# Transposes on TensorE, a regrouped first FFN2 and other buffers in the last chunk of a fused attention and SwiGLU kernel

## The chip, the cores and the metric

The kernel runs on one core of a Trainium2 chip. The metric is device time in microseconds (us), as a median over executions of the whole program. Executions of one kernel mostly agree within about 1%, but some fall into a slower state (345.35 us against 335.1 for the kernel before). Each run also reports the mean clock granted to TensorE, as a share of full speed.

## The reference, cut to what matters

```python
# q, k, v: (8 batches, 8 heads, 576 positions, 64)
scores = 0.125 * q @ k.T, kept where |i - j| <= 32
attn   = softmax(scores) @ v
x      = attn laid out as (4608 tokens, 512)
out    = (silu(x @ w_gate) * (x @ w_val)) @ w_out      # d_ff = 1536
```

## The kernel before

The 4608 tokens are 36 pairs of 64-row windows (a "pair" is 128 tokens) and 9 chunks of 512 tokens (four pairs each), numbered from 0. For each chunk TensorE computes FFN1 (12 units of gate and value products), then FFN2. Attention of later pairs is threaded into FFN2. Chunk 0's FFN2 is plain; chunks 1 to 8 use a seven-product scheme with the steps p1, p2, p6, p5, p7, p3, p4, which needs sums of blocks of `hT` (on VectorE) and of `w_out` (on GpSimd, once). Each pair's attention output `x16` has to be transposed into `xT` before FFN1 of its chunk can start.

```python
def pair_mask(m):                       # VectorE, both operands in SBUF
    nc.vector.tensor_tensor(out=flat, in0=flat, in1=mask, op=ALU.mult)

def pair_xt(m, on_pe=False, pool=None, cast=None):
    ...
    if not on_pe:
        nc.sync.dma_start_transpose(out=dst, in_=x16)
        return
    ...                                 # four TensorE transposes, then a copy out of PSUM

# end of the first FFN2
ffn2_sub(0, 3, 0); pair_xt(4, True, ...); pair_xt(5, True, ...)
ffn2_sub(0, 3, 1); pair_xt(6, True, ...); pair_xt(7, True, ..., cast_dve)
pair_av(8); pair_xt(8); load_v(2, range(5))
wino_weights()                          # GpSimd: 4 subtractions and 2 casts of 128x1536

# last chunk (split): x in ps_a (two buffers, also used by FFN1), z in ps_c (one buffer)
# outputs: tiles "osb2", 3 buffers
for j in range(1, NCH):
    ffn1(j)
    if j == NCH - 2: good = check_range()
    if j == NCH - 1: set_flag(good)     # 'cnt' in ps_c, read by VectorE into 'flag'
    ffn2(j, ...)
```

Each engine works through its instructions in the order of the program: in the changed kernel's trace the copy of `xT` starts at 63.63, behind a mask product on VectorE, though the transposes that it reads ended at 58.84. The flag decides at the end whether a slow general path must run; it never does here.

## Time and profile before

| | kernel before |
|---|---|
| median time | 335.27 us (335.13 to 345.35, 3 runs) |
| span of the profiled execution | 333.8 us |
| TensorE busy | 312.6 us, 94% |
| TensorE waits on transposed x | 4.1 us, at the starts of chunks 2, 3, 4 |
| first FFN2 | 44.06 to 60.64 us |
| last output copy ends | 328.01 us |
| granted clock | 0.992 |

TensorE carries the kernel from start to end, so the places that matter are those where it stands still with work left. The prediction shows those lines. Columns are start, duration (us), engine, source line, operation, result and operands.

```profile
55.29 0.69 DVE L316 TENSOR_TENSOR p_t<-p_t,mask 128x1024 f16<-128x1024 f16 x1 [1.61 <-ACT p_t L312]
56.36 3.12 POOL L457 TENSOR_TENSOR w_top<-wo 128x1536 f16<-128x1536 f16 x1
```

In the kernel before, pair 8's mask is done at 55.98, just 0.4 us before GpSimd starts on the weight sums, which last until 71.9.

### The profile page before, as it was taken

How to read it: one execution, taken by the hardware profiler on the slowest of the kernel's cores; microseconds unless marked ns; L12 is line 12 of the kernel's file. 1: busy time of each engine (PE TensorE's matmuls, PEld its weight loads, DVE VectorE, ACT ScalarE, POOL GpSimd, SP SyncE). 2: the span in 40 equal slices, each digit the busy share in tenths (PEclk: the TensorE clock that was granted, in tenths of full speed). 3: DMA queues.
4: the chain of work that ended last, by engine and by line, in shares of the span. 5: the costliest groups of instructions: out<-in, count | busy, mean ns of one | idle time of the engine just before them, and what ended most of it. 6: DMA issues, size and time to landing. Idle time of an engine off the chain costs nothing. (4 is left out here: it accounts for less than half of the span.)

```text
span 333.8 us, 7176 instructions
## 1 busy us (share of the span) xinstructions
PE 312.6 (94%) x2868; PEld 181.1 (54%) x2868; DVE 201.6 (60%) x409; ACT 162.2 (49%) x247; POOL 121.1 (36%) x145
## 2 busy tenths in 40 slices
PE   6789998999989998999799999999999999899990
PEld 3444554445844584448444864486448644754480
DVE  3743366347846684868477767686668566634740
ACT  3864579476743475337433753374337623223320
POOL 8972888997405620355046403460000000000000
PEclk9999999999999999999999999999999999999996
DMA  7999999869989998999699979997621510020012
GB/s 278 173 210 304 217 162 186 145 99 141 130 171 140 116 100 190 116 140 120 159 130 146 102 163 121 152 120 157 115 53 33 141 33 1 33 94 1 2 66 69
DMA packets 157000, 41.96 MB, mean 126 GB/s; under 512 B 140576, under 2 KB 154400, under 8 KB 156960
## 3 DMA queue, kind: packets, MB, share of 16 engines
q0 software_dynamic: 100640, 16.52, 68.8%
q1 hardware_dynamic: 56320, 24.92, 32.5%
q8 instruction: 24, 0.39, 0.5%
q14 instruction: 16, 0.13, 0.1%
HBM read 37.75 MB, written 9.44 MB: 141 GB/s over the span
## 5 line engine op out<-in xcount | busy, mean ns | idle before, releaser
L423 DVE TENSOR_TENSOR hT<-ssb,gv_ps 128x512 f16<-128x512 f16 x108 | 74.3, 688 | 92.0 <-ACT ssb L422 91.6
L422 ACT ACTIVATE ssb<-gv_ps 128x512 f16<-128x512 f32 x108 | 64.5, 597 | 123.5 <-PE gv_ps L416 121.8
L416 PE MATMUL gv_ps<-xT,wg 128*128 128x512 f16 x432 | 111.0, 380 | 5.3 <-DMA xT<-x 4.1
L416 PE MATMUL gv_ps<-xT,wv 128*128 128x512 f16 x432 | 110.9, 379 | 0.0
L416 PEld LDWEIGHTS <-wg 128*128 128x128 f16 x432 | 41.3, 98 | 53.4 <-issue 6.1
L416 PEld LDWEIGHTS <-wv 128*128 128x128 f16 x432 | 42.3, 98 | 51.0
L223 POOL DMA_DIRECT2D tok<-in_q_dram x30 | 25.5, 849 | 64.2 <-DMA qT<-tok 45.7
L312 ACT ACTIVATE p_t<-s_ps 128x1024 f16<-128x1024 f32 (+1 forms) x40 | 34.8, 924 | 13.3 <-PE s_ps L306 13.3
L223 POOL DMA_DIRECT2D tok<-in_k_dram x30 | 25.3, 842 | 15.9 <-DMA kT<-tok 13.1
L499 PEld LDWEIGHTS <-hT 128*128 128x128 f16 x288 | 27.6, 98 | 5.7 <-issue 0.7
L499 PEld LDWEIGHTS <-s_top 128*128 128x128 f16 x288 | 27.6, 98 | 4.8 <-DVE s_top L471 1.1
L386 DVE TENSOR_TENSOR x<-o_ps,rall 128x512 f16<-128x512 f32 (+1 forms) x39 | 25.4, 650 | 1.3
L499 PE MATMUL x_ps<-w_top,s_top 128*128 128x256 f16 x192 | 23.8, 273 | 0.9 <-DVE s_top L471 0.9
L316 DVE TENSOR_TENSOR p_t<-p_t,mask 128x1024 f16<-128x1024 f16 x32 | 20.9, 687 | 4.2 <-ACT p_t L312 3.5
L242 POOL DMA_DIRECT2D v<-in_v_dram x24 | 21.3, 902 | 0.5 <-DMA tok<-in_q_dram 0.5
L471 DVE TENSOR_TENSOR s_top<-hT 128x768 f16<-128x768 f16 (+2 forms) x48 | 20.1, 418 | 0.0
L265 DVE COPY v<-v 64x512 f16<-64x512 f16 x46 | 15.5, 337 | 1.4
L685 ACT ACT_TABLE_LOAD x12 | 15.4, 1283 | 0.2
L368 PEld LDWEIGHTS <-p_t 128*64 128x64 f16 x576 | 10.7, 110 | 6.6 <-issue 4.7
L368 PE MATMUL o_ps<-v,p_t 128*64 128x66 f16 x576 | 12.9, 196 | 0.7 <-DVE p_t L352 0.7
L527 DVE TENSOR_TENSOR osb<-y_ps,kept 128x512 f32<-128x512 f32 (+1 forms) x16 | 10.5, 655 | 4.8 <-ACT p_t L312 4.0
L262 ACT ACTIVATE kept<-x_ps 128x512 f32<-128x512 f32 (+1 forms) x18 | 9.6, 531 | 6.9 <-PE x_ps L499 6.9
(81 smaller groups left out, 270.8 us busy)
## 6 DMA issues: line engine op xcount, KB each, us to landing
out_dram<-osb SPq DMA_DIRECT2D x32, 256.0 KB, 2.5
v<-in_v_dram POOLq DMA_DIRECT2D x24, 128.0 KB, 5.2
tok<-in_q_dram POOLq DMA_DIRECT2D x24, 128.0 KB, 5.0
tok<-in_k_dram POOLq DMA_DIRECT2D x24, 128.0 KB, 5.5
qk_st<-in_q_dram SPq DMA_DIRECT2D x4, 576.0 KB, 7.0
qk_st<-in_k_dram SPq DMA_DIRECT2D x4, 576.0 KB, 8.9
v<-in_v_dram POOLq DMA_DIRECT2D x16, 96.0 KB, 5.2
wo<-in_moe_w_out_dram POOLq DMA_DIRECT2D x4, 384.0 KB, 21.5
```

Source lines behind the costliest of these rows:

```text
L223: nc.gpsimd.dma_start(out=t[0:n].rearrange("p (h d) -> p h d", d=D), in_=src[b].rearrange("h s d -> s h d")[128 * m:128 * m + n])
L242: nc.gpsimd.dma_start(out=dst[:, 2 * m, :, 0:D], in_=src[128 * m - 32:128 * m + 96])
L265: nc.vector.tensor_copy(out=o, in_=i)
L312: nc.scalar.activation(out=o, in_=s, func=AF.Exp, bias=0.0, scale=1.0 / float(D) ** 0.5)
L316: nc.vector.tensor_tensor(out=flat, in0=flat, in1=mask, op=ALU.mult)
L368: nc.tensor.matmul(out=o[h // 4][64 * i:64 * i + 64, 66 * (h % 4):66 * (h % 4) + 66], lhsT=p[:, place(b, h)[0], i, place(b, h)[1], :], rhs ...
L386: nc.vector.tensor_tensor(out=x16s[m][:, a], in0=ov[:, :, :, 0:D], in1=r.unsqueeze(3).to_broadcast([128, a.stop - a.start, 4, D]), op=ALU. ...
L416: nc.tensor.matmul(out=gv[:, i, :], lhsT=w[:, g, 128 * fk:128 * fk + 128], rhs=xts[j][:, g, :], start=(g == 0), stop=(g == GS - 1))
L422: nc.scalar.activation(out=ssb, in_=gv[:, 0, :], func=AF.Silu, bias=0.0, scale=1.0)
L423: nc.vector.tensor_tensor(out=hts[j][:, fk, :], in0=ssb, in1=gv[:, 1, :], op=ALU.mult)
L471: tt = lambda o, a, b, op: nc.vector.tensor_tensor(out=o, in0=a, in1=b, op=op)
L499: nc.tensor.matmul(out=dst[n], lhsT=lhs[:, f, 128 * n:128 * n + 128], rhs=rhs[:, f, :], start=(first and f == 0 and (split or n == 0)), st ...
```

## The change

The intent has three parts. Transposes that are urgent at the end of chunks 1 to 3 go to TensorE in place of the DMA. The attention inside the first FFN2 is regrouped so that no copy is waited for. The last chunk gets PSUM buffers that FFN1 doesn't hold, and eight output buffers (for room, its `kept` tiles are joined; not shown).

```diff
+        tp = pool.tile([128, len(ms), GS, 128], FP16, tag=..., name="xt_ps")
+        for n, x in enumerate(x16):
+            for g in range(GS):
+                nc.tensor.transpose(out=tp[:, n, g, :], in_=x[:, 128 * g:128 * g + 128], identity=ident)
+        cast(dst.rearrange("p g (n t) -> p n g t", t=128), tp)
 ... last chunk
-            x = [ps_a.tile([128, 256], FP32, tag="a", name="x_ps") for _ in range(2)]
+            x2 = ps_c.tile([128, 2, 512], FP32, tag="c", name="x_ps")
-            z2 = ps_c.tile([128, 2, 512], FP32, tag="c", name="z_ps")
+            z = [ps_a.tile([128, 256], FP32, tag="a", name="z_ps") for _ in range(2)]
-                               tag="osb" if n is None else "osb2", name="osb")
+                               tag="osb" if n is None else "osb2", name="osb",
+                               bufs=3 if n is None else 8)
 ... first FFN2 (the earlier groups are cut)
-    pair_scores(8)
+    pair_scores(7, ps_c)
+    ex8 = pair_scores(8, None, False)          # not masked here
+    ex8()
+    ffn2_sub(0, 2, 1)
     nc.scalar.activation(... dummy, Silu ...)
-    ffn2_sub(0, 2, 1)
-    pair_av(6)
-    pair_av(7, ps_a)
+    turn_x([4, 5, 6], ps_a, cast_act)
     ffn2_sub(0, 3, 0)
-    ... (four transposes of pairs 4 to 7)
+    pair_av(7)
+    pair_mask(8)
     ffn2_sub(0, 3, 1)
-    ...
-    pair_av(8)
-    pair_xt(8)
+    turn_x([7], ps_a, cast_dve)
 ... ends of chunks 1 to 3
+        urgent = {1: (1, 2), 2: (1, 2), 3: (1,)}.get(j, ())
         st["p3"]()
+        if urgent:
+            turn_x([todo[i] for i in urgent], ps_a, cast_dve)
         st["c12"]()
```

More of the change, by code (lines that the diff above doesn't have):

```diff
@@ L389, in pair_norm, with pair_xt, turn_x @@
                                     op=ALU.mult)
-    def pair_xt(m, on_pe=False, pool=None, cast=None):
-        j, i4 = divmod(m, 4)
+    def pair_xt(m):
+        turn_x([m], None)
+    def turn_x(ms, pool, cast=None):
+        j, i4 = divmod(ms[0], 4)
         if j not in xts:
             xts[j] = xtpool.tile([128, GS, 512], FP16, tag="xt", name="xT")
-        dst = xts[j][:, :, 128 * i4:128 * i4 + 128]
-        x16 = x16s.pop(m).rearrange("p a h d -> p (a h d)")
-        if not on_pe:
-            nc.sync.dma_start_transpose(out=dst, in_=x16)
+        dst = xts[j][:, :, 128 * i4:128 * (i4 + len(ms))]
+        x16 = [x16s.pop(m).rearrange("p a h d -> p (a h d)") for m in ms]
+        if pool is None:
+            nc.sync.dma_start_transpose(out=dst, in_=x16[0])
             return
-        pool, tag = pool or (ps_o, "o")
-        tp = pool.tile([128, GS, 128], FP16, tag=tag, name="xt_ps")
-        for g in range(GS):
-            nc.tensor.transpose(out=tp[:, g, :], in_=x16[:, 128 * g:128 * g + 128],
-                                identity=ident)
-        (cast or cast_act)(dst, tp)
+        tp = pool.tile([128, len(ms), GS, 128], FP16,
+                       tag={ps_a: "a", ps_c: "c", ps_o: "o"}[pool], name="xt_ps")
+        for n, x in enumerate(x16):
+            for g in range(GS):
+                nc.tensor.transpose(out=tp[:, n, g, :], in_=x[:, 128 * g:128 * g + 128],
+                                    identity=ident)
+        cast(dst.rearrange("p g (n t) -> p n g t", t=128), tp)
     hts = {}
@@ L481, in wino_steps @@
         if split:
-            x = [ps_a.tile([128, 256], FP32, tag="a", name="x_ps") for _ in range(2)]
+            x2 = ps_c.tile([128, 2, 512], FP32, tag="c", name="x_ps")
+            x = [x2[:, 0, 0:256], x2[:, 1, 0:256]]
             y = [ps_o.tile([128, 256], FP32, tag="o", name="y_ps") for _ in range(2)]
-            z2 = ps_c.tile([128, 2, 512], FP32, tag="c", name="z_ps")
-            z = [z2[:, 0, 0:256], z2[:, 1, 0:256]]
+            z = [ps_a.tile([128, 256], FP32, tag="a", name="z_ps") for _ in range(2)]
             parts = (0, 1)
@@ L504, in keep_act @@
         def keep_act(name, src):
+            t = opool.tile([128, 2, 256], FP32, tag="kept", name="kept", bufs=3)
             for n in parts:
-                t = kept[(name, n)] = opool.tile([128, 2, 256] if n is None else [128, 256], FP32,
-                                                 tag="kept" if n is None else f"kept{n}",
-                                                 name="kept", bufs=3)
-                cast_act(t, views(src, n))
+                kept[(name, n)] = t if n is None else t[:, n]
+                cast_act(kept[(name, n)], views(src, n))
         def send(n, o, i, c):
@@ L634 @@
     for m in range(4):
-        pair_xt(m, True)
+        turn_x([m], ps_o, cast_act)
     c16 = [cast_qk(t, cast_pool) for t in st]
@@ L650 @@
     ffn2_sub(0, 0, 0)
-    pair_scores(4)
-    pair_scores(5)
-    ffn2_sub(0, 0, 1)
     shift_v(1, 0, cast_dve)
     shift_v(1, 1, cast_dve)
-    ffn2_sub(0, 1, 0)
+    pair_scores(4, ps_c)
+    pair_scores(5)
     pair_scores(6)
-    pair_scores(7)
+    ffn2_sub(0, 0, 1)
     shift_v(1, 2, cast_act)
     shift_v(1, 3, cast_act)
+    ffn2_sub(0, 1, 0)
     load_qk(2)
@@ L664 @@
     pair_av(5, ps_a)
+    pair_av(6, ps_a)
     ffn2_sub(0, 2, 0)
-    pair_scores(8)
+    pair_scores(7, ps_c)
+    ex8 = pair_scores(8, None, False)
+    ex8()
+    ffn2_sub(0, 2, 1)
     nc.scalar.activation(out=dummy, in_=rall[0:1, 0, 0:1], func=AF.Silu, bias=0.0, scale=1.0)
-    ffn2_sub(0, 2, 1)
-    pair_av(6)
-    pair_av(7, ps_a)
+    turn_x([4, 5, 6], ps_a, cast_act)
     ffn2_sub(0, 3, 0)
-    pair_xt(4, True, (ps_a, "a"))
-    pair_xt(5, True, (ps_a, "a"))
+    pair_av(7)
+    pair_mask(8)
     ffn2_sub(0, 3, 1)
-    pair_xt(6, True, (ps_a, "a"))
-    pair_xt(7, True, (ps_a, "a"), cast_dve)
-    pair_av(8)
-    pair_xt(8)
+    turn_x([7], ps_a, cast_dve)
     load_v(2, range(5))
     wino_weights()
-    carried = []
+    carried = [8]
     def table(func):
@@ L736, in norm @@
                 pair_norm(todo[i])
-                pair_xt(todo[i])
+                if i not in urgent:
+                    pair_xt(todo[i])
         if n:
```

## The prediction

> **What bounds the kernel now.** I first read busy time by engine on the page, then who TensorE waits for, then the order of time around each wait.
>
> ```profile
> PE 312.6 (94%) x2868; PEld 181.1 (54%) x2868; DVE 201.6 (60%) x409; ACT 162.2 (49%) x247; POOL 121.1 (36%) x145
> ```
>
> TensorE is busy 312.6 of 333.8 us; no other engine passes 60%. Busy is not the same as peak, but it says that time can be won only where TensorE stands still, or after its last matmul. The view of waits for TensorE lists all such places with a releaser:
>
> ```profile
> PE gv_ps L416 <- DMA xT<-x: 4.1, 3, 1.7
> PE warm L552 <- DVE mask L202: 2.9, 1, 2.9
> PE gv_ps L416 <- ACT xT L262: 1.1, 2, 0.7
> PE xt_ps L403 <- DVE x L386: 0.9, 1, 0.9
> ```
>
> The change aims at lines 1, 3 and 4 (2 is the start, untouched). The timeline shows the three waits of line 1 at the start of FFN1 of chunks 2, 3, 4; here are the first and last:
>
> ```profile
> 91.65 1.47 PE L499 MATMUL x_ps<-ws_rest,hT 128*128 128x256 f16 x12
> 94.34 1.02 PE L416 MATMUL gv_ps<-xT,wg 128*128 128x512 f16 x4 [1.22 <-DMA xT<-x]
> ...
> 160.35 1.47 PE L499 MATMUL x_ps<-ws_rest,hT 128*128 128x256 f16 x12
> 163.50 0.81 PE L416 MATMUL gv_ps<-xT,wg 128*128 128x512 f16 x3 [1.67 <-DMA xT<-x]
> ```
>
> A product of 12 matmuls takes 1.31 us from its start to the next one's (289.28 onward in the chain), so the gaps are 94.34 - 91.65 - 1.31 = 1.38, for chunk 3 (126.00 to 128.67) 1.36, and 163.50 - 160.35 - 1.31 = 1.84 us: 4.58 together. Chunks 5 to 8 show none of size there.
>
> The first FFN2 runs from 44.06 to 60.64 and waits twice near its end:
>
> ```profile
> 57.72 0.40 PE L403 MATMUL xt_ps<-ident,x 128*128 128x128 f16 x4 [0.92 <-DVE x L386]
> 57.96 1.46 PE L430 MATMUL ob<-wo,hT 128*128 128x512 f16 x6
> 59.25 0.61 PE L403 MATMUL xt_ps<-ident,x 128*128 128x128 f16 x8
> 59.79 0.45 PE L368 MATMUL o_ps<-v,p_t 128*64 128x66 f16 x16
> 60.64 1.02 PE L416 MATMUL gv_ps<-xT,wg 128*128 128x512 f16 x4 [0.40 <-ACT xT L262]
> ```
>
> The tail, around the last chunk's first product and its last outputs:
>
> ```profile
> 315.37 0.19 PE L571 MATMUL cnt<-ones,good 128*1 128x1 f32 x2
> 315.49 0.83 PE L499 MATMUL x_ps<-wo,hT 128*128 128x256 f16 x6
> 316.85 0.81 PE L499 MATMUL x_ps<-wo,hT 128*128 128x256 f16 x6 [0.53 <-DVE hT L423]
> 317.38 0.14 DVE L572 TENSOR_SCALAR flag<-cnt 1x1 int32<-1x1 f32 x1
> 324.05 1.48 PE L499 MATMUL x_ps<-ws_rest,hT 128*128 128x256 f16 x12
> 325.25 0.38 ACT L262 ACTIVATE osb<-x_ps 128x256 f32<-128x256 f32 x1 [2.97 <-DMA out_dram<-osb]
> 327.63 0.38 ACT L262 ACTIVATE osb<-x_ps 128x256 f32<-128x256 f32 x1 [1.99 <-DMA out_dram<-osb]
> ```
>
> Two separate costs: the second half of p1 waits for the gate product that frees its PSUM buffer (0.70 us from 316.15), and the last output copy waits until 327.6 for an output buffer (three exist) although its matmuls ended near 325.5. From that copy's end (328.01) to the end of the span, 5.8 us are a transfer and the fixed end.
>
> **What the Trainium skill says.** "VectorE: DVE Perf Modes", section "The three transpose paths": a 128x128 transpose takes 390 ns on TensorE and 1309 ns through the DMA crossbar, but TensorE's lands in PSUM. The trace agrees in direction: four transposes are spaced by 0.24 us here (57.72 to 57.96), while one DMA transpose of a 128x512 tile occupies the SP queue 1.22 us and lands 2.4 to 6.2 us after issue. "DMA: Bandwidth & Descriptors", section "Rules for kernel authors", wants a transfer issued early and waited for late; at these three boundaries no time lies between. "Perfetto Trace Analysis", section "Optimization Strategy", reads bubbles that repeat as too little SBUF or PSUM for the next tile; that fits the output buffers in the tail, not the xT waits, which are data.
>
> **The change, part by part.** (1) *Boundaries.* In chunks 1 and 2 two pairs, in chunk 3 one, are turned on TensorE after p3, with one DVE copy. Eight transposes take 0.54 us (59.25 to 59.79), four 0.24 to 0.27. The DVE copy of two pairs: 0.43 us for 128x512, and by the slope of DVE's 2-byte tiles (419 ns at 512, 687 at 1024) some 0.70 for 128x1024, an estimate. For chunk 1: p3 issues until 91.64, transposes until 92.18, p4 until 93.49; DVE is through with the mask at 92.18 and copies about 92.4 to 93.1, so the copy hides under p4. FFN1 starts at 93.49 in place of 94.34: 0.85 won. Chunk 2 the same way: 1.36 - 0.54 = 0.82. Chunk 3: 1.84 - 0.27 = 1.57, but the other pair still comes by DMA: issued at 157.85, and where transfers landed 4.2 us after issue in this stretch it lands at 162.05, against p4's end at 161.93; I take 1.45. Sum 3.1 us of the 4.6.
>
> (2) *First FFN2.* Its order is now scores 4-6, three FFN2 halves, AV 4-6, a half, scores 7-8, a half, 12 transposes, a half, AV 7, a half, four transposes; pair 8's AV moves into FFN1. I step TensorE through it with the spacings of before: 1.29 per half (1.40 where scores or AV follow), scores 0.81 (three pairs) and 0.58 (two), AV 0.89 (three) and 0.38 (one), transposes 0.80 (12) and 0.27. From 44.06: scores at 45.45, AV at 50.24, scores at 52.53, 12 transposes at 54.41, AV 7 at 56.55, last transposes at 58.25. At each I checked the feeders. DVE's third normalisation ends about 53.35, before 54.41; the wide ScalarE copy (slope 597 to 1005 ns per 512 to 1024 elements, so 1.41 us at 1536) runs about 57.0 to 58.4, after the table load; pair 7's normalisation ends at 58.0, just before 58.25. Only the last wait stays: transposes end 58.64, copy 58.7 to 59.1, FFN1 at 59.2. That is 1.44 earlier, but pair 8's AV now costs FFN1 0.47 (99.52 to 99.99 shows one). Net 1.0.
>
> (3) *Last chunk.* Eight output buffers remove both waits of ScalarE. But x now lies in the PSUM pool that has one buffer, and the count for the range flag lies in that same buffer. The listing of the changed kernel has p1's first matmul wait on DVE once; its reader to wait for is the flag, which DVE reaches at 317.38, behind all sums of FFN1. So p1, which had half its work done before 316.85, starts whole at about 317.55, and every product is 1.36 us later (p4 at 325.41 in place of 324.05). Its end is 326.72, last copies 326.92 to 327.58: 0.43 before the old 328.01. Against that, the last two outputs go out about 0.3 us apart and share the engines; outputs sent close together took 2.8 us to land at 324.70, alone perhaps 2.1 (an estimate from the traffic after 328). Net about 0.1, and I would not wonder at zero.
>
> Sum: 3.1 + 1.0 + 0.1 = 4.2 us. 335.27 - 4.2 = 331.0.
>
> **Rivals.** *The flag wait is not there* (the DVE wait is only for hT): then p1 starts near 315.5, p4 ends near 325.0, the tail wins about 2 us and the time is 329.2. For it: the change was made to win there. Against: one buffer, with cnt allocated before x. *The DMA that stays becomes the wait*: one pair per boundary still goes by DMA, and at chunk 3 its landing is the critical one; if it lands as late as the 6.2 us worst, it leaves up to 2 us at one boundary: 333. Against: those queues now carry fewer transposes. *VectorE becomes the wait*: the new copies sit before c12 and the masks on an in-order engine; if the copy is 1.4 us (single-rate PSUM reading, twice my estimate) it ends after p4, near 93.8, and 0.3 us comes back at two boundaries: 331.6. For it: the span from c22 to c12 is already solid on DVE. *First FFN2 gains nothing*, because a copy comes later than stepped: 332. The last start has only 0.25 us of slack.
>
> **Range and chances.** The parts may err by: boundaries 0.6, first FFN2 0.6, tail -0.6 to +1.8. I give 329.6 to 332.4. Faster by over 2% means under 328.6, which needs all parts at their best and the flag rival too: 0.04. Slower by over 2% has no mechanism: 0.01.
>
> **What would show it.** Right: no TensorE wait on DMA xT at chunks 2 and 3, at most 0.3 us at 4; FFN1 of chunk 1 near 59.2; p1 of the last chunk starting after the flag, with some 2 us of idle TensorE before it and no ScalarE wait on output DMAs. Wrong: p1 starting at once, a DVE release ahead of FFN1, or a wait of q and k transposes at scores.

## The result, and the profile after

The changed kernel takes 339.31 us in the median (338.03 to 340.30, 4 runs) against 335.92 for the kernel before with the added run of these rounds. The ratio is 1.0106, with a 95% interval of 1.0063 to 1.0149. A ratio here is the mean time of one kernel's fast runs over that of the other's fast runs in the same rounds, so it isn't quite the ratio of the medians. The change was expected to win 4.2 us and lost about 3.6, which is under 2% but clear of the noise.

The waits of TensorE in the changed kernel (releaser; us in total, times, longest) show where to look:

```profile
PE gv_ps L421 <- DVE xT L265: 5.3, 1, 5.3
...
PE x_ps L504 <- DVE flag L577: 2.0, 1, 2.0
```

All waits on the DMA for xT are gone, as meant. Two others have come: one of 5.3 us on VectorE's copy of xT, and one of 2.0 us on the flag. The second was predicted, the first wasn't. The page's row of granted clock, one digit per fortieth of the span, differs too; before and after:

```profile
PEclk9999999999999999999999999999999999999996
```

```profile
PEclk9999999699999999999999999999999999999987
```

The 6 is the slice from 59 to 68 us. Here is the timeline of the changed kernel at that place:

```profile
56.98 3.12 POOL L462 TENSOR_TENSOR w_top<-wo 128x1536 f16<-128x1536 f16 x1
...
57.49 0.69 DVE L386 TENSOR_TENSOR x<-o_ps,rall 128x512 f16<-128x512 f32 x1
58.10 5.60 DVE L316 TENSOR_TENSOR p_t<-p_t,mask 128x1024 f16<-128x1024 f16 x1
...
58.45 0.39 PE L408 MATMUL xt_ps<-ident,x 128*128 128x128 f16 x4
...
60.03 3.12 POOL L462 TENSOR_TENSOR w_wide<-wo 128x1536 f32<-128x1536 f16 x1
...
63.21 1.82 POOL L268 CAST w_top<-w_wide 128x1536 f16<-128x1536 f32 x1
...
63.63 0.41 DVE L265 COPY xT<-xt_ps 128x512 f16<-128x512 f16 x1
...
64.10 1.89 PE L421 MATMUL gv_ps<-xT,wg 128*128 128x512 f16 x4 [5.26 <-DVE xT L265]
```

Pair 8's mask product is listed with 5.60 us; in the kernel before all 32 of its line take 0.68 to 0.69. It starts 1.1 us into GpSimd's first weight sum and ends 0.5 us after GpSimd has changed from its second sum to the cast. The normalisation just before it (`x`), which has one operand in PSUM, ran beside the same sum in 0.69 us, its length elsewhere too. GpSimd's cast, which began while the mask was still running, took 1.82 us in place of 1.46 (the next one, at 68.28). The copy of xT stands behind the mask on VectorE, and FFN1 stands behind the copy. When FFN1 starts, four matmuls take 1.68 us from group to group (64.10 to the next group at 65.78) instead of 0.86: TensorE runs at half speed until about 68.0. The trace's granted clock fell from 1.00 to 0.50 at 61.2, still in the wait.

The boundaries at which the transposes moved look as planned. This is chunk 2's:

```profile
97.54 0.61 PE L408 MATMUL xt_ps<-ident,x 128*128 128x128 f16 x8
97.99 1.47 PE L504 MATMUL x_ps<-ws_rest,hT 128*128 128x256 f16 x12
99.30 1.03 PE L421 MATMUL gv_ps<-xT,wg 128*128 128x512 f16 x4
```

FFN1 follows p4 after 1.31 us, without a gap. The last chunk:

```profile
317.55 0.19 PE L576 MATMUL cnt<-ones,good 128*1 128x1 f32 x2
...
319.56 0.14 DVE L577 TENSOR_SCALAR flag<-cnt 1x1 int32<-1x1 f32 x1
...
319.75 1.91 PE L504 MATMUL x_ps<-wo,hT 128*128 128x256 f16 x12 [2.01 <-DVE flag L577]
...
321.45 2.74 PE L504 MATMUL y_ps<-wo,hT 128*128 128x256 f16 x12
```

p1 waits for the flag, 2.2 us after the count. And p1 and p2 take 1.70 and 2.56 us from start to start in place of 1.31 each, again at the low clock.

With these points the difference can be booked (us from the start of each profile; the third column is the run `e3_both`, below):

| point | before | changed | both moves |
|---|---|---|---|
| FFN1 of chunk 1 starts | 60.64 | 64.10 | 59.19 |
| p1 of chunk 1 | 81.43 | 87.33 | 80.48 |
| FFN1 of chunk 2 | 94.34 | 99.30 | 92.46 |
| FFN1 of chunk 3 | 128.67 | 132.71 | 125.87 |
| FFN1 of chunk 4 | 163.50 | 165.92 | 159.08 |
| p4 of the last chunk | 324.05 | 329.27 | 318.70 |
| last output copy ends | 328.01 | 331.44 | 320.87 |
| span | 333.8 | 338.0 | 327.2 |

The changed kernel is 3.46 us behind at the first line and 5.90 at the second. Of the 2.44 between, pair 8's AV takes 0.47 and the rest, 1.97, goes to the low clock (the three groups at low clock take 1.93 more than three at full clock). The boundaries then win 0.94, 0.92 and 1.62. From the count to p4 of the last chunk the changed kernel loses 3.04 (11.72 against 8.68).

### The profile page after: what moved, and what is told of

Read it like the earlier page. It is cut to its first block, busy times and chain, and to the rows that moved or that the text cites. A ratio compares the mean times of both kernels' runs of the same rounds, so it can differ in the third digit from the quotient of the medians.

```text
span 338.0 us, 7194 instructions
## 1 busy us (share of the span) xinstructions
PE 316.1 (94%) x2888; PEld 183.7 (54%) x2888; DVE 206.9 (61%) x412; ACT 161.9 (48%) x245; POOL 121.9 (36%) x145
## 5 line engine op out<-in xcount | busy, mean ns | idle before, releaser
L504 PEld LDWEIGHTS <-hT 128*128 128x128 f16 x288 | 28.3, 100 | 7.6 <-issue 2.0
L316 DVE TENSOR_TENSOR p_t<-p_t,mask 128x1024 f16<-128x1024 f16 x32 | 25.9, 841 | 1.6 <-ACT p_t L312 0.9
L265 DVE COPY v<-v 64x512 f16<-64x512 f16 x46 | 14.8, 321 | 1.6
L504 PE MATMUL x_ps<-wo,hT 128*128 128x256 f16 x96 | 12.2, 279 | 2.0 <-DVE flag L577 2.0
```

Source lines behind the costliest of these rows:

```text
L265: nc.vector.tensor_copy(out=o, in_=i)
L504: nc.tensor.matmul(out=dst[n], lhsT=lhs[:, f, 128 * n:128 * n + 128], rhs=rhs[:, f, :], start=(first and f == 0 and (split or n == 0)), st ...
```

## The experiments

My theory after the result had three parts. First, VectorE's product of two SBUF operands is held while GpSimd reads SBUF. The Trainium skill states this ("SBUF — State Buffer", section "Who interferes with whom"): a VectorE instruction with two inputs in SBUF contends with a GpSimd instruction that reads SBUF, since the second input comes through a port that the two share, and the loser waits. The runs below agree that it waits (0.68 us against 5.60) and differ on how long (last section). Second, one-buffer PSUM: x waits for the flag that reads the count. Third, idle TensorE is paid twice, because its clock drops. "TensorE: Matmul & The Clock Gate", section "What's actually happening", has an idle window of about 3.4 us after which half the clock is given, for about as long. The traces agree on the second figure in the last chunk (0.50 from 320.6 to 324.0, 3.4 us; 6.8 us, from 61.2 to 68.0, where the wait itself went on) and differ on the first (last section). Rivals: the mask is slow for another reason (the transfers of that stretch, or the new order), and the slow matmuls come from late data.

All eleven runs gave correct outputs. The times, with the fast runs of the kernel before in the same rounds as the measure; the last column is (ratio - 1) x 336 us:

| run | median us | ratio (95%) | against before |
|---|---|---|---|
| changed kernel | 339.31 | 1.0106 (1.0063 to 1.0149) | +3.6 |
| e1_mask_early | 332.33 | 0.9865 (0.9789 to 0.9941) | -4.5 |
| e2_flag_early | 336.33 | 0.9979 (0.9927 to 1.0032) | -0.7 |
| e3_both | 329.38 | 0.9774 (0.9723 to 0.9825) | -7.6 |
| e4_before_late_mask | 342.06 | 1.0169 (1.0112 to 1.0226) | +5.7 |
| e5_gpsimd_after_mask | 331.81 | 0.9885 (0.9845 to 0.9925) | -3.9 |
| e6_fill_first | 336.98 | 1.0039 (0.9996 to 1.0082) | +1.3 |
| e7_fill_tail | 339.42 | 1.0108 (1.0075 to 1.0141) | +3.6 |
| e8_boundaries_only | 332.19 | 0.9892 (0.9864 to 0.9920) | -3.6 |
| e9_buffers_only | 335.39 | 0.9975 (0.9937 to 1.0013) | -0.8 |

No run was timed side by side with the changed kernel; where one is compared with it below, the comparison goes through these ratios.

**The mask moved ahead of GpSimd's work.**

```diff
     ex8()
+    pair_mask(8)
...
     pair_av(7)
-    pair_mask(8)
```

> The changed kernel with one line moved: pair 8's mask product runs directly after its exponentials (about 55.3 us), before GpSimd starts on the weight sums (56.98), in place of 58.10 in the middle of them. Theory (VectorE's product of two SBUF operands is held as long as GpSimd works on SBUF): the mask takes 0.69 us in place of 5.60, the copy of xT comes at about 58.9, FFN1 of chunk 1 starts at 59.5 in place of 64.10, TensorE keeps its full clock there, together 6.5 us less: about 332.8. Rival 1 (the mask was long for another reason, such as the transfers of that stretch): it stays several us long at its new place and the time stays near 339. Rival 2 (only the wait goes, the slow clock after it has another cause): 334.7.

The timeline of this run, at the mask, at FFN1 of chunk 1 and at the last chunk's p1:

```profile
54.93 0.69 DVE L316 TENSOR_TENSOR p_t<-p_t,mask 128x1024 f16<-128x1024 f16 x1 [0.22 <-ACT p_t L312]
...
59.04 1.04 PE L421 MATMUL gv_ps<-xT,wg 128*128 128x512 f16 x4 [0.52 <-DVE xT L265]
...
313.34 1.47 PE L504 MATMUL x_ps<-wo,hT 128*128 128x256 f16 x12 [2.02 <-DVE flag L577]
```

The mask is short, FFN1 starts at 59.04 (59.2 had been predicted for the changed kernel), and the clock stays up there. The ratio is 8.1 us better than the changed kernel's, where 6.5 was expected. Part of the surplus is the third line: after the same 2.0 us wait p1 ran at full clock in this profile. At chunk 4 a wait of 0.40 us on the remaining DMA transpose showed; the prediction had allowed 0.3.

**The flag moved ahead of the last FFN1.**

```diff
     for j in range(1, NCH):
+        if j == NCH - 1:
+            set_flag(good)
         ffn1(j)
...
-        if j == NCH - 1:
-            set_flag(good)
```

> The changed kernel with the count for the range flag moved ahead of the last chunk's FFN1, so that the one-buffer PSUM pool is free when the last chunk's first product wants it. Theory (x waits for the flag in its own buffer, and the idle time then halves the clock): no TensorE wait on the flag, p1 starts within 0.1 us of the last gate product, p2 after it at full clock, 3.7 us less: about 335.6. Rival (the wait is really for the gate product of unit 11, which p1's buffer or data needs): p1 still starts only after VectorE's product of unit 11, some 1.4 us after the last FFN1 matmul, and the gain is under 2.5 us. The first FFN2 is unchanged: 5.3 us wait there.

The last group of FFN1 and p1 in this run:

```profile
318.67 1.03 PE L421 MATMUL gv_ps<-xT,wv 128*128 128x512 f16 x4
319.54 1.47 PE L504 MATMUL x_ps<-wo,hT 128*128 128x256 f16 x12
```

There is no wait at all before p1, so p1 needed nothing else, and the rival (unit 11's product) falls. Against the changed kernel this run is 4.3 us better (3.7 expected). The first FFN2 still waits 6.1 us here, as it should. At chunk 4 TensorE waited 0.97 us for the pair that still comes by DMA:

```profile
167.78 1.04 PE L421 MATMUL gv_ps<-xT,wg 128*128 128x512 f16 x4 [0.97 <-DMA xT<-x]
```

**Both moves.** The edits are the two above.

> Both moves of the two runs before. If the two causes are independent the gains add: 339.3 - 6.5 - 3.7 = 329.1, some 6 us or 1.9% under the kernel before (my prediction's 331.0 less the 2 us that the flag wait took from the tail). If one of them hides behind the other, or if the transfers become the bound, 331 or more.

The median is 329.38 us, and this version beats both kernels: 2.3% under the kernel before (1.7 to 2.8). Apart the two moves win 8.1 and 4.3 us on the changed kernel, together 11.2, so within the intervals (about 2 us) the two causes add. The table of points above has its profile. FFN1 of chunk 1 starts at 59.19, and p4 of the last chunk 5.35 us earlier than before.

**The late mask put into the kernel before.**

```diff
-    pair_scores(8)
+    ex8 = pair_scores(8, None, False)
+    ex8()
...
     pair_av(7, ps_a)
+    pair_mask(8)
     ffn2_sub(0, 3, 0)
```

> The kernel before with only pair 8's mask product moved behind the normalisation of pair 7, so that it falls among GpSimd's weight sums (from 56.4 us). Theory: the mask is held for 3 to 6 us (until GpSimd's second sum ends near 62.6, if it misses the change of instruction at 59.4), FFN1 of chunk 1 starts near 63.6 in place of 60.64 and starts at the low clock: 338 to 340.5. Rival (the change's new PSUM copies or order are the cause, not the place of the mask): mask 0.69 us, time within 0.5 us of the kernel before.

The timeline of this run:

```profile
56.55 3.13 POOL L457 TENSOR_TENSOR w_top<-wo 128x1536 f16<-128x1536 f16 x1
...
56.84 6.44 DVE L316 TENSOR_TENSOR p_t<-p_t,mask 128x1024 f16<-128x1024 f16 x1
```

Without any other part of the change the mask takes 6.44 us, FFN1 starts near 63.7 at the low clock (here TensorE waits 4.2 us in pair 8's AV, which reads the mask), and the kernel loses 5.7 us. That is a little more than the 3 to 5 expected. The place of this one product among GpSimd's sums is enough.

**GpSimd told to wait for the mask.** VectorE and TensorE keep the changed kernel's order. One tiny copy makes GpSimd start after the mask.

```diff
+    hold = const.tile([128, 1], FP16, name="hold")
+    cast_pool(hold, pts[8][:, 1, 1, HP - 1, 63:64])
     wino_weights()
```

> The changed kernel with nothing moved on VectorE or TensorE; GpSimd first copies one column of pair 8's masked tile, so that its weight sums begin only after that mask. Theory (VectorE is held by GpSimd's work): the mask at about 58.1 takes 0.69 us, FFN1 of chunk 1 starts near 59.6, the weight sums end near 74.7 in place of 72.8, time about 332.8 as with the early mask. Rival (the mask's place in VectorE's order, or what its tile waits for, makes it long): it stays at 5.6 us and the time near 339.

```profile
57.42 0.68 DVE L316 TENSOR_TENSOR p_t<-p_t,mask 128x1024 f16<-128x1024 f16 x1
...
58.31 3.09 POOL L462 TENSOR_TENSOR w_top<-wo 128x1536 f16<-128x1536 f16 x1
...
58.67 1.04 PE L421 MATMUL gv_ps<-xT,wg 128*128 128x512 f16 x4 [0.52 <-DVE xT L265]
```

The same product at the same place in VectorE's order takes 0.68 us. Nothing but GpSimd's timing was changed, so the mask's length came from GpSimd's work beside it. The run is 7.4 us better than the changed kernel (6.5 expected).

**Idle matmuls in the first wait.** `idle_mms(24)` stands behind `turn_x([7], ...)`.

> The changed kernel with 24 idle 128x512 matmuls (0.215 us apart, 5.2 us) behind pair 7's transposes, in the 5.3 us in which TensorE waits for xT. Theory (idle time of that length halves the clock, and the slow matmuls are a cost of their own): FFN1 still starts near 64.1, but its first eight matmuls come 0.215 us apart and not 0.43, so that all after it is 1.9 us earlier: 337.4, granted clock about 0.985. Rival (the slow matmuls come from weights or data that arrive slowly, as GpSimd or DMA is busy): they stay slow, time 339.3.

```profile
59.13 5.34 PE L557 MATMUL warm<-mask 128*128 128x512 f16 x24
...
65.30 1.04 PE L421 MATMUL gv_ps<-xT,wg 128*128 128x512 f16 x4 [0.82 <-DVE xT L265]
```

FFN1 is not earlier than in the changed kernel, but its first group of four takes 1.04 us in place of 1.89, and the ratio is 2.3 us better (1.9 expected). The low clock is a separate cost that follows the idle time, and useless work in its place avoids it.

**Idle matmuls in the wait for the flag.** `idle_mms(8)` stands behind `set_flag(good)`.

> The changed kernel with 8 idle 128x512 matmuls (1.7 us) between the count and the last chunk's first product, in its 2.0 us wait for the flag. Theory (the wait costs 1.36 us against before and the low clock after it another 1.7): p1 starts when it did, p1 and p2 take 1.31 us each in place of 1.70 and 2.56, the end comes 1.6 us earlier: 337.7. Rival (that stretch is slow for another cause): no change.

```profile
21.31 1.82 PE L421 MATMUL gv_ps<-xT,wg 128*128 128x512 f16 x4 [0.69 <-ACT xT L262]
...
321.61 1.47 PE L504 MATMUL x_ps<-wo,hT 128*128 128x256 f16 x12 [0.18 <-DVE flag L577]
```

In its profile p1 and p2 take 1.31 us each after the fill, as expected, and from the count to p4 it is 10.06 us in place of 11.72: 1.66 less, as expected. But the time is the changed kernel's (339.42 against 339.31). The profile shows where the gain went: FFN1 of chunk 0, long before the fill, began at the low clock (first line; its first groups are 1.62 and 1.71 us apart in place of 0.86), which lost 1.7 us, and the first wait was 6.0 us in place of 5.3. No wait in the 6 us before that FFN1 was over 1.1 us, so a single long wait isn't the whole rule of the clock. Why the other three runs, which have no profile, gained nothing either stays open.

**The early-mask kernel and the changed kernel once more**, for the same question, one execution each.

> The early-mask kernel a second time, to see how regular the low clock after the 2.0 us wait for the flag is: it was absent in that kernel's first profile and present in the changed kernel's. Theory (it depends on where the idle stretch falls for the clock control, not on the kernel): p1 and p2 may take 1.31 us or up to 2.6 us, wait of 2.0 us either way. Rival (this kernel never has it): 1.31 us again.

> The changed kernel a second time, for the same question and for the spread of the first wait: wait for xT 5.3 to 6.1 us, low clock after it surely (idle over 5 us), low clock after the 2.0 us wait for the flag perhaps; 338 to 340.5.

The early-mask kernel's second profile:

```profile
313.31 1.75 PE L504 MATMUL x_ps<-wo,hT 128*128 128x256 f16 x12 [2.02 <-DVE flag L577]
314.86 2.77 PE L504 MATMUL y_ps<-wo,hT 128*128 128x256 f16 x12
```

This time the same kernel has the low clock after the same 2.02 us wait, and takes 332.76 us. The changed kernel's second execution has it too (340.16 us, first wait 5.6 us). Of the six profiles with that wait unfilled, four show the low clock (the changed kernel twice, `e6_fill_first`, `e10_mask_early_again`) and two don't (`e1_mask_early`, `e5_gpsimd_after_mask`). The timed runs of `e5_gpsimd_after_mask` split in the same way: 330.50 and 330.98 us at a granted clock of 0.993, and 332.63 and 333.11 us at 0.989 and 0.988. So this stretch of 2.2 us idle is long enough to lose the clock in some executions, by about 2 us. In the profiles the count to p4 takes 11.72 or 11.73 us with the low clock and 10.06 or 10.07 without. The granted clock is still 1.00 at the end of the wait and falls 2.6 to 3.3 us after the count, when p1 is already running (in the changed kernel at 320.6, 0.9 us into p1). What decides it in one execution isn't shown.

**Only the transposes at the boundaries, on the kernel before.** The edit is the `turn_x` function and the `urgent` lines of the change.

> The kernel before with only the transposes on TensorE at the ends of chunks 1 to 3. By the changed kernel's trace this part won 0.94, 0.92 and 1.62 us: 3.5 us in all, so 335.3 - 3.5 = 331.8, with no TensorE wait on xT at chunks 2 to 4. Rival (the gain came only because that kernel ran late against its transfers): a wait of 0.3 to 1 us on the remaining xT transfer stays at chunk 4, and the time is 332.5 or more.

The ratio gives 3.6 us, the expected 3.5. There is no wait on xT at chunks 2, 3 or 4.

**Only the eight output buffers, on the kernel before.** The edit is `bufs=8` and the joined kept tiles.

> The kernel before with only the eight output buffers of the last chunk (and its kept tiles joined, for room), PSUM placement untouched. Theory (the last copy's wait for an output buffer is 2.06 us of the end, of which some 0.5 us returns because the last two transfers then overlap): p1 keeps its 0.5 us wait for unit 11's product, ScalarE waits for no transfer, about 1.5 us less: 333.9. Rival (the end is bound by transfers): no change.

The last copy ends at 326.22, with p4 at 324.33; before, it ended at 328.01 with p4 at 324.05. So 2.1 us of waiting went. But from that copy to the end of the span it is 7.1 us here and 5.8 before: most of it comes back. SyncE issued the last transfer only at 327.7, 1.5 us after its copy, right behind an issue of 1.73 us (0.33 to 0.35 is usual); before, it was issued at 328.0. The ratio's 0.8 us lies within its interval of noise; 1.5 was expected.

Not run alone: the regrouped first FFN2 and the new places in PSUM. What they are worth is read only from the table of points.

## Why the prediction was wrong

**Boundaries.** Right in mechanism and size. The working gave 0.85, 0.82 and 1.45; the changed kernel's profile shows 0.94, 0.92 and 1.62, and alone the part is worth 3.6 us against a predicted 3.1. Eight transposes took 0.45 us there (97.54 to 97.99) where I had 0.54; the copy of 128x1024 took 0.69 for an estimated 0.70.

**First FFN2: the step that failed** is "Only the last wait stays: transposes end 58.64, copy 58.7 to 59.1, FFN1 at 59.2". TensorE's part of the stepping held (its last transposes came at 58.45 for 58.25, in a profile whose first FFN2 began 0.28 us later). VectorE's didn't. The list of feeders went from pair 7's normalisation at 58.0 straight to the copy at 58.7 and gave the mask of pair 8 between them no line. At its usual 0.69 us it would just have fitted. I never looked at what GpSimd does at that moment, because at 36% busy it was no bound. The runs showed the mask held to 5.60 us by GpSimd's sums, and FFN1 at 64.10. With the mask earlier or GpSimd later, FFN1 started at 59.04 and 58.67, so the rest of the stepping was right. With both moves FFN1 starts 1.45 us earlier than before and p1 of chunk 1, after pair 8's AV, 0.95 (1.44 and 1.0 predicted). The page that states the contention (named above) I didn't look up.

**The clock** was missing altogether. The prediction counted an idle microsecond as one microsecond. After the wait of 5.3 us, some 4 us ran at half speed, which cost 1.97 us more. After 2.2 us idle, the same happened in four of six profiles.

**Last chunk.** The flag's wait was right: p1 starts after it, and in `e1_mask_early`, where the clock stayed up, p4 comes 10.06 us after the count against 8.68 before, so 1.38 later (1.36 predicted). In the changed kernel's profile the low clock made it 3.04. The other half was right too: the last copy came 1.79 us nearer to p4 (1.36 + 0.43 in the working). I let some 0.3 us come back from the last two transfers running together; from the last copy to the end of the span it is 5.8 us before and 5.9 to 6.6 in the nine profiles with the changed tail, so 0.1 to 0.8 came back. With the buffers alone, in `e9_buffers_only`, it was 1.3.

**Sum.** Predicted was -4.2. The profile has +4.2 in the span: +3.46 at FFN1 of chunk 1, +2.44 for its slow start and pair 8's AV, -3.48 at three boundaries, -0.24 at later ones, +3.04 in the last chunk, -1.79 for the output buffer's wait, and +0.8 after the last copy.

**Rivals.** "The first FFN2 gains nothing" was nearest, but had a copy some tenths late in mind. "VectorE becomes the wait" named the right engine with the wrong instruction and place. Both lay inside the range (332 and 331.6), but only because a few tenths were meant; a wait of several us had no place in it. "The DMA that stays becomes the wait" came true in part: 0.40 and 0.97 us at chunk 4 in two of the ten profiles with these boundaries (`e1_mask_early`, `e2_flag_early`), none in the others. "The flag wait is not there" fell: the wait is 2.0 us in all six profiles that keep the changed order and have no fill there. The chance of slower by over 2% had "no mechanism", though the measured loss of 1.1% needed one that the profile and the skill both held.

## What to carry to other kernels

When an instruction moves on one engine, list everything that the engine does between the feeder and the reader at the new place, and look at what GpSimd does in the same microseconds: a VectorE product of two SBUF tiles beside a GpSimd operation on SBUF can cost many times its length (5.60 us for 0.69 here). Check a moved tile's new buffer for its last user; a scalar count in a one-buffer pool held up the whole last chunk until `set_flag` was moved. And an idle stretch of TensorE can cost more than its length: 1.66 us more after 2.2 us in the last chunk, when the clock fell, and 1.97 us more after the wait of 5.3 us.

## What the Trainium skill lacked or had wrong

- "SBUF — State Buffer" has the loser blocked for the other's whole instruction. Here it was longer: the mask was held through the rest of the first GpSimd sum and the whole of the next (5.60 us, with sums of 3.12 us each), and so in all six profiles where it fell among the sums (5.60 to 6.46 us). A run of GpSimd instructions back to back can hold VectorE past the first of them.
- "TensorE: Matmul & The Clock Gate" gives an idle window of about 3.4 us before the clock drops. Here 2.2 us of idle time, with two tiny matmuls at its start, was enough in four of six profiles; the 1.84 us gap before chunk 4 of the kernel before was not.
- "VectorE: DVE Perf Modes" lists 390 ns for a TensorE transpose and gives no spacing for several in a row. Issued one after another, twelve took 0.68 us from the first to the next matmul (54.70 to 55.38), or 57 ns each.
